# Attention in chunks of 120 keys with the global keys beside them, ahead of a squared-ReLU MLP, with TensorE's order written by hand

## The chip, the cores and the metric

The kernel runs on one core of a Trainium2 chip. The metric is the device time of one execution in microseconds; lower is better. A core has engines with an instruction row each: TensorE (PE; its weight loads are shown apart as PEld), VectorE (DVE), ScalarE (ACT), GpSimd (POOL) and SyncE (SP, which here only issues transfers). A matmul takes its operands from the on-chip memory SBUF, with the contraction on the 128 partitions, and writes to one of eight PSUM banks of 512 fp32 columns; the other engines carry results back to SBUF.

## The reference

Attention with a band of 32 keys on either side of each query and 8 global tokens that see every key and that every query sees, then an MLP with a squared ReLU. 8 batches, 8 heads, 576 tokens, 64 dimensions a head; 4608 tokens, 512 model dimensions, 2048 hidden ones.

```python
scores = scale * np.matmul(q, k.transpose(0, 1, 3, 2))
pos = np.arange(S)
mask = np.abs(pos[:, None] - pos[None, :]) <= window      # 32
is_global[global_idx] = True                              # 8 of 576
mask = mask | is_global[:, None] | is_global[None, :]
scores = np.where(mask, scores, -1000000000.0)
attn = np.exp(scores - np.max(scores, axis=-1, keepdims=True))
attn = attn / (np.sum(attn, axis=-1, keepdims=True) + 1e-09)
x = np.matmul(attn, v).transpose(0, 2, 1, 3).reshape(B * S, H * D)
r = np.maximum(x @ w_in, 0.0)
out = (s * (r * r) + b) @ w_out
```

Inputs and output are fp32. Both kernels compute in bf16 with fp32 sums in PSUM, leave out the subtraction of the maximum, and split the last line in two: s is multiplied into w_out once, and b times the column sums of w_out is a row that is added to each output (`bias_row`).

## The kernel before

**Attention.** For each batch GpSimd issues transfers that cast q and k of all heads to bf16 copies in DRAM (`emit_scratch`, L157 and L161); SP then loads them with a transposing transfer as `qT` and `kT`, 128 rows for a pair of heads. GpSimd copies the 8 global columns of each, one column an instruction, by a register that holds the index (L294). v is loaded in fp32 in the natural order and cast on ScalarE into `vbf`, which has a 65th column of ones for the softmax's denominator.

A head is then worked by itself, on 64 of the 128 rows of the contraction: scores of the global keys against all queries (`pgk`, L311 to L313), scores of five chunks of 128 keys against a window of up to 192 queries and against the 8 global queries (`ps_s`, L327 and L332, two chunks to a PSUM tile), Exp on ScalarE (L315, L316, L338), the band mask on VectorE (L342), 13 value matmuls into `po` (L352 to L379), the denominator's row by Ln, spread to 64 rows by two matmuls with ones (L386, L390), Exp of its negative, the product on VectorE (L397). The results of the global queries stand in eight extra columns; GpSimd copies each over its token's column (L399, eight copies a head), and SP sends the head's 64 x 576 tile into `xT`, four tiles that hold x transposed for all 4608 tokens.

**MLP.** Chunks of 512 tokens, nine in all. A chunk has 20 units: 16 of the first layer, four matmuls of 512 columns each into `psh` (L216), with ReLU (L221) and square (L222) on VectorE into `g`; and four of the second layer, 16 matmuls into `pso` (L229), an addition of the bias row (L234) and the transfer out. After each head the code emits its share of the units whose tokens are there; in the text a chunk's tokens are there when the batch that ends them is through.

**Order.** The scheduler of the tile framework lays each engine's instructions in a row and sets the semaphores; an instruction that waits holds all behind it on its engine. `ps_m` has two banks for the units, `ps_a` two for scores, `ps_o` two tiles for values. The weights are loaded in 20 transfers and cast on VectorE after the first head (`prep_weights`), where TensorE also sums the columns of w_out in 16 fp32 matmuls (L188).

## Time and profile before

| | |
|---|---|
| three runs | 585.25, 587.22, 588.34 us; median 587.22 |
| the profiled execution | span 585.2 us from its first instruction to its last |
| TensorE | busy 492.7 us, 84%; 2968 matmuls on record |
| VectorE, ScalarE, GpSimd | 296.8, 228.3 and 226.2 us (51, 39 and 39%) |
| mean granted clock of TensorE | 0.942 of full speed |
| DMA | 51.52 MB, 88 GB/s over the span |

A busy share is an average over the span, and stages differ. The profile also gives the busy time in 40 slices and in any window, the clock that TensorE was granted there, each group of instructions with the idle time ahead of it and what ended that, and the chain of work that ended last, followed back from the last instruction.

### The profile page before, as it was taken

The page shows a single profiled execution, that of the slowest core. Times are in us where ns is not written, and L with a number is a line of the kernel's source. Part 1 is how long each engine was busy: PE and PEld are TensorE (multiplying, and loading weights), DVE is VectorE, ACT ScalarE, POOL GpSimd, SP SyncE. Part 2 cuts the span into 40 slices and gives each one's busy share as a digit, 9 for nine tenths or more (in the row PEclk, how much of TensorE's full clock was granted, in tenths as well). Part 3 has the DMA queues.
Part 4 walks back from the last instruction along what each step waited for, and adds up shares of the span by engine and source line. Part 5 has one row for each costly group of instructions (what it writes and reads, how often), then busy time and mean ns, then how long its engine had stood idle before and what let it go on. Part 6 is the DMA issues. An engine that isn't in the chain of part 4 may idle for free.

```text
span 585.2 us, 10109 instructions
## 1 busy us (share of the span) xinstructions
PE 492.7 (84%) x2968; PEld 230.8 (39%) x3016; DVE 296.8 (51%) x655; ACT 228.3 (39%) x473; POOL 226.2 (39%) x1061
## 2 busy tenths in 40 slices
PE   0147205986999999999999999999999999999997
PEld 0023102432444445444444444444444444444443
DVE  4314002332673576367537744763666367448481
ACT  2023101372454455455555545564455455420000
POOL 4938660277263255316433442553223113310000
PEclk9999656965999999999999999999989999999999
DMA  7999999566322422352243225122400100110101
GB/s 225 160 275 158 157 158 194 164 108 136 49 51 70 122 52 37 88 116 43 53 116 77 37 73 142 33 57 68 123 16 12 65 28 12 34 65 0 73 0 72
DMA packets 164166, 51.52 MB, mean 88 GB/s; under 512 B 152848, under 2 KB 156944, under 8 KB 163600
## 3 DMA queue, kind: packets, MB, share of 16 engines
q1 hardware_dynamic: 90032, 41.45, 28.8%
q0 software_dynamic: 74080, 9.44, 25.2%
q8 instruction: 23, 0.38, 0.3%
q14 instruction: 31, 0.25, 0.1%
HBM read 36.71 MB, written 18.87 MB: 95 GB/s over the span
## 4 chain that ended last, share of the span: by engine, by line
PE 65%; issue 13%; POOL 12%; DMA 3%; DVE 3%; ACT 2%; POOLq 1%; ACTq 0%
PE psh L216 22%; PE pso L229 19%; PE ps_s L327 6%; PE po L362 4%; POOL qsc L157 3%; PE po L386 3%; PE po L352 3%; PE pgk L311 2%; POOL ksc L161 2%; POOL qgT L294 2%; POOL stage L399 2%; POOL kgT L294 2%; DMA xT<-stage 2%; PE po L367 2%; PE po L379 1%
## 5 line engine op out<-in xcount | busy, mean ns | idle before, releaser
L399 POOL COPY stage<-stage 64x1 bf16 x512 | 111.0, 217 | 200.5 <-DVE stage L397 172.5
L216 PE MATMUL psh<-xT,win_t 128*128 128x512 bf16 x545 | 159.3, 390 | 9.3 <-DMA xT<-stage 6.4
L229 PE MATMUL pso<-wout_t,g 128*128 128x512 bf16 x559 | 135.9, 380 | 0.2
L221 DVE TENSOR_SCALAR g<-psh 128x512 bf16<-128x512 f32 x144 | 97.8, 686 | 55.2 <-PE psh L216 53.8
L385 ACT ACTIVATE rsb<-po 1x584 bf16<-1x584 f32 x64 | 41.5, 648 | 122.9 <-PE po L379 122.6
L338 ACT ACTIVATE e<-ps_s 128x368 bf16<-128x368 f32 (+2 forms) x192 | 73.3, 407 | 40.5 <-PE ps_s L332 35.8
L342 DVE TENSOR_TENSOR emc<-e,m 128x368 bf16<-128x368 bf16 (+2 forms) x192 | 53.8, 304 | 59.5 <-ACT e L338 56.2
L229 PEld LDWEIGHTS <-g 128*128 128x128 bf16 x576 | 52.9, 98 | 61.0 <-issue 8.0
L216 PEld LDWEIGHTS <-win_t 128*128 128x128 bf16 x576 | 47.8, 98 | 60.1 <-issue 26.1
L397 DVE TENSOR_TENSOR stage<-po,rep 64x584 bf16<-64x584 f32 x64 | 48.5, 758 | 36.4 <-ACT rep L395 23.4
L315 ACT ACTIVATE egk<-pgk 8x512 bf16<-8x512 f32 x64 | 37.5, 587 | 71.8 <-PE pgk L311 41.0
L234 DVE TENSOR_TENSOR osb<-pso,bias_row 128x512 f32<-128x512 f32 x36 | 24.9, 692 | 78.5 <-PE pso L229 76.4
L294 POOL COPY qgT<-qT 128x1 bf16 x256 | 41.0, 316 | 60.7 <-DMA qT<-qsc 42.8
L327 PE MATMUL ps_s<-qT,kT 64*128 64x192 bf16 (+2 forms) x320 | 57.7, 244 | 5.4 <-ACT e L338 3.2
L222 DVE TENSOR_TENSOR g<-g 128x512 bf16<-128x512 bf16 x144 | 57.6, 418 | 1.9
L362 PE MATMUL po<-emc,vbf 128*65 128x160 bf16 (+2 forms) x320 | 47.9, 240 | 1.1 <-DVE emc L342 1.1
L327 PEld LDWEIGHTS <-kT 64*128 64x128 bf16 (+1 forms) x320 | 31.2, 98 | 43.5 <-issue 40.8
L395 ACT ACTIVATE rep<-po 64x584 bf16<-64x584 f32 x64 | 41.7, 652 | 16.9 <-PE po L390 15.9
L188 PE MATMUL ps_b<-wt,onesf 128*128 128x512 f32 x32 | 21.8, 834 | 30.3 <-DMA wt<-in_moe_w_out_dram 30.3
L311 PE MATMUL pgk<-qT,kgT 64*8 64x512 bf16 x64 | 25.5, 399 | 24.2 <-POOL kgT L294 23.7
L332 PE MATMUL ps_s<-qgT,kT 64*128 64x8 bf16 (+1 forms) x320 | 45.5, 169 | 0.0
L362 PEld LDWEIGHTS <-vbf 128*65 128x65 bf16 (+1 forms) x320 | 33.3, 114 | 30.3 <-issue 10.0
(56 smaller groups left out, 441.9 us busy)
## 6 DMA issues: line engine op xcount, KB each, us to landing
out_dram<-osb SPq DMA_DIRECT2D x36, 256.0 KB, 2.1
vnat<-in_v_dram SPq DMA_DIRECT2D x32, 256.0 KB, 4.3
xT<-stage SPq DMA_DIRECT2D x64, 72.0 KB, 2.0
wt<-in_moe_w_in_dram SPq DMA_DIRECT2D x4, 1024.0 KB, 7.9
wt<-in_moe_w_out_dram SPq DMA_DIRECT2D x16, 256.0 KB, 3.1
qsc<-in_q_dram POOLq DMA_DIRECT2D x7, 576.0 KB, 10.9
ksc<-in_k_dram POOLq DMA_DIRECT2D x7, 576.0 KB, 11.9
vnat<-in_v_dram SPq DMA_DIRECT2D x8, 128.0 KB, 4.9
```

The source lines that it names most:

```text
L216: nc.tensor.matmul(psh[:], win_t[:, a, f * P : f * P + P], xT[a][:, c0 : c0 + 512], start=(a == 0), stop=(a == 3),)
L221: nc.vector.tensor_scalar_max(g[:], psh[:], 0.0)
L222: nc.vector.tensor_mul(g[:], g[:], g[:])
L229: nc.tensor.matmul(pso[:], gT[f][:, uu * P : uu * P + P], wout_t[:, f], start=(f == 0), stop=(f == 15),)
L294: nc.gpsimd.tensor_copy(out=dstG[:, i : i + 1], in_=dstT[:, ds(greg_p[i], 1)])
L327: nc.tensor.matmul(ps_s[: MC[c], off : off + WN[c]], kT[r : r + D, P * c : P * c + MC[c]], qT[r : r + D, WLO[c] : WHI[c]],)
L332: nc.tensor.matmul(ps_s[: MC[c], off + WN[c] : off + WN[c] + NG], kT[r : r + D, P * c : P * c + MC[c]], qgT[r : r + D, :],)
L338: nc.scalar.activation(e[:nr, :tot], ps_s[:nr, :tot], AF.Exp, scale=SCALE)
L342: nc.vector.tensor_mul(emc[:nr, :tot], e[:nr, :tot], bmask[gi][:nr, :tot])
L362: nc.tensor.matmul(po[:65, lo:hi], VX(c), EM(c, 0, hi - lo), start=False, stop=(c == NCH - 1),)
L397: nc.vector.tensor_mul(stage[0:64, :], po[0:64, :], rep[64:128, :])
L399: nc.gpsimd.tensor_copy(out=stage[0:64, ds(greg_p[i], 1)], in_=stage[0:64, S + i : S + i + 1],)
```

## The change

**Keys.** A chunk is now 120 keys of the band and, in rows 120 to 127, the 8 global keys, so that a batch has 5 x 128 = 640 columns (`LQ`). The queries lie in the same 640 columns: 60, the 8 global ones, 60. The tokens' rows come from fp32 loads in the natural order (`load`, five transfers for a half batch of each of q, k, v); the global rows of all batches are gathered once into DRAM (`gather`, 24 transfers on ScalarE's queue) and copied in by one transfer a half batch (`fill_globals`). No copy of q or k goes by DRAM in bf16, and there is no transposing transfer.

**Casts and transposes.** GpSimd casts k, q and v (`cast`; in batch 0 VectorE casts k and q). TensorE transposes a pair of heads, 5 + 5 matmuls against the identity (`trans_k`, `trans_q`), and VectorE copies the result to SBUF. The queries' copy goes into a block-diagonal tile: head 0 in rows 0 to 63 and columns 0 to 639, head 1 in rows 64 to 127 and columns 640 to 1279, zeros elsewhere, so that one matmul gives a chunk's scores for both heads on all 128 rows of the contraction.

**Values and norm.** The five score tiles of a pair (`pss`) share two banks with the transposes (`pst`). `vx` has 64 columns of ones beside each head's values, so that the denominators stand in 64 rows of `po`; Ln and Exp go over 64 x 1280 at once, and no matmul spreads them. `po` takes three banks, one tile for all pairs. The global queries' parts are added over the five chunks (`gsum`), and GpSimd copies them over their tokens' columns once a batch, eight copies of four pairs each (`finish_batch`).

**MLP.** `xt` is a tile for each batch, three in turn. A chunk that straddles two batches takes its columns from two tiles, with two matmuls where there was one. ReLU moves to ScalarE (L428), the square stays on VectorE. The units have three banks. Weights come in 8 transfers of 1 MB; GpSimd casts and scales them and sums w_out's tiles, and one matmul sums its columns (L481).

**Order.** TensorE's and SP's rows stand as the code is written. `Q` hands out the MLP in quanta (a unit of the first layer, or a quarter of one of the second), eight between the steps of a pair; a chunk is handed out during the batch after the one that ends it. So a batch's first two pairs lie beside the first layer and the last two beside the second.

```diff
-MC = [min(P, S - P * c) for c in range(NCH)]
-WLO = [max(0, P * c - WIN) for c in range(NCH)]
-WHI = [min(S, P * c + MC[c] + WIN) for c in range(NCH)]
-WN = [WHI[c] - WLO[c] for c in range(NCH)]
+KC = 120
+HB = 60
+LQ = NCH * P
+LO = [0] + [P * c - WIN for c in range(1, NCH)]
+HI = [P * c + P + WIN for c in range(NCH - 1)] + [LQ]
+W = [HI[c] - LO[c] for c in range(NCH)]
...
+    ctx.enter_context(tc.manual_schedule(engines={ET.PE, ET.SP}))
...
+    xtp = ctx.enter_context(tc.tile_pool(name="xtp", bufs=3))
+    dramp = ctx.enter_context(tc.tile_pool(name="dramp", bufs=1, space=bass.MemoryType.DRAM))
+    ps_s = ctx.enter_context(tc.tile_pool(name="ps_s", bufs=2, space=bass.MemoryType.PSUM))
+    ps_o = ctx.enter_context(tc.tile_pool(name="ps_o", bufs=1, space=bass.MemoryType.PSUM))
+    ps_m = ctx.enter_context(tc.tile_pool(name="ps_m", bufs=3, space=bass.MemoryType.PSUM))
...
+    def load(bi, t, h0, nh):
+        src = NATSRC[t]
+        d = nat_tile(t, h0 // HG)
+        a = h0 % HG
+        for c in range(NCH):
+            n = min(KC, S - KC * c)
+            nc.sync.dma_start(
+                out=d[0:n, c, a : a + nh],
+                in_=src[bi, h0 : h0 + nh, KC * c : KC * c + n].rearrange("h s d -> s h d"),
+            )
...
+    def gather(eng, t, regs):
+        for i in range(NG):
+            eng.dma_start(
+                out=gsc[t][:, i], in_=NATSRC[t][:, :, ds(regs[i], 1), :].rearrange("b h o d -> b (h o) d")
+            )
...
+    for t in ("k", "q", "v"):
+        gather(nc.scalar, t, greg_a)
+    for half in range(2):
+        for t in ("k", "q", "v"):
+            load(0, t, HG * half, HG)
+            fill_globals(nc.scalar, 0, t, half)
...
+    def cast(bi, half, eng_k, eng_q, eng_v):
+        kt, qt = cast_k[bi], cast_q[bi]
+        hs = slice(HG * half, HG * half + HG)
+        eng_k(out=kt[:, :, hs], in_=nat_tile("k", half)[:])
+        eng_q(out=qt[:, :, hs], in_=nat_tile("q", half)[:])
+        eng_v(out=vbufs[bi % NV][:, :, hs, 0:D], in_=nat_tile("v", half)[:])
...
+    def trans_k(p):
+        bi, hp = divmod(p, 4)
+        ps = ps_s.tile([P, LQ], BF16, tag="s", name="pst")
+        src = cast_k[bi].rearrange("p c h d -> p c (h d)")
+        for c in range(NCH):
+            nc.tensor.transpose(
+                ps[:, P * c : P * c + P], src[:, c, P * hp : P * hp + P], ident[:]
+            )
+        kt = ktp.tile([P, LQ], BF16, tag="kt", name="kt")
+        nc.vector.tensor_copy(out=kt[:], in_=ps[:])
+        ktile[p] = kt
...
+    def trans_q(p):
+        bi, hp = divmod(p, 4)
...
+        qt = qbufs[p % NQ]
+        for hh in range(2):
+            r = slice(D * hh, D * hh + D)
+            nc.vector.tensor_copy(
+                out=halves(qt[r, hh]),
+                in_=ps[r].rearrange("p (c j) -> p c j", c=NCH)[:, :, 0:KC].rearrange(
+                    "p c (a j) -> p c a j", a=2
+                ),
+            )
+            nc.vector.tensor_copy(
+                out=qt[r, hh].rearrange("p (c j) -> p c j", c=NCH)[:, :, HB : HB + NG],
+                in_=ps[r].rearrange("p (c j) -> p c j", c=NCH)[:, :, KC:P],
+            )
...
+    def qk(p, c):
+        kt, qt = ktile[p], qbufs[p % NQ]
+        ps = ps_s.tile([P, 2, W[c]], FP32, tag="s", name="pss")
+        nc.tensor.matmul(
+            ps[:], kt[:, P * c : P * c + P], qt[:, :, LO[c] : HI[c]]
+        )
+        e = emp.tile([P, 2, W[c]], BF16, tag="e", name="e", bufs=3)
+        nc.scalar.activation(e[:], ps[:], AF.Exp, scale=SCALE)
+        em = emp.tile([P, 2, W[c]], BF16, tag=f"em{c}", name=f"em{c}")
+        nc.vector.tensor_mul(em[:], e[:], masks[c][:])
+        emt[(p, c)] = em
...
+        po = ps_o.tile([P, 2 * LQ], FP32, tag="o", name="po")
+        started = set()
+        for hh in range(2):
+            for c in range(NCH):
+                lo, hi = LO[c], HI[c]
+                while lo < hi:
+                    a = hh * LQ + lo
+                    bank = a // 512
+                    n = min(hi - lo, 512 * (bank + 1) - a)
+                    nc.tensor.matmul(
+                        po[:, a : a + n], vx[:, c, 2 * hp + hh, :],
+                        emt[(p, c)][:, hh, lo - LO[c] : lo - LO[c] + n],
+                        start=bank not in started, stop=(hh == 1 or c == NCH - 1),
+                        skip_group_check=True,
+                    )
+                    started.add(bank)
+                    lo += n
...
+    def norm(p):
+        bi, hp = divmod(p, 4)
+        po = otile[p]
+        xt, gs = xts[bi], gsums[bi]
+        ln = nrm.tile([P, 2 * LQ], FP32, tag="ln", name="ln", bufs=1)
+        nc.scalar.activation(ln[D:P], po[D:P], AF.Ln)
+        rep = nrm.tile([P, 2 * LQ], FP32, tag="rep", name="rep")
+        nc.scalar.activation(rep[D:P], ln[D:P], AF.Exp, scale=-1.0)
+        nc.vector.tensor_reduce(
+            out=gs[:, hp],
+            in_=po.rearrange("p (h c j) -> p h j c", h=2, c=NCH)[:, :, HB : HB + NG, :],
+            axis=AX.X, op=OP.add,
+        )
+        for hh in range(2):
+            nc.vector.tensor_tensor(
+                out=xt[D * hh : D * hh + D, hp].rearrange("p (c a j) -> p c a j", c=NCH, a=2),
+                in0=halves(po[0:D, hh * LQ : hh * LQ + LQ]),
+                in1=halves(rep[D:P, hh * LQ : hh * LQ + LQ]), op=OP.mult,
+            )
+    def finish_batch(bi):
+        xt, gs = xts[bi], gsums[bi]
+        rec = nrm.tile([P, 4, 2, NG], FP32, tag="rec", name="rec", bufs=1)
+        nc.vector.reciprocal(out=rec[0:D], in_=gs[D:P])
+        xg = nrm.tile([P, 4, NG], BF16, tag="xg", name="xg", bufs=2)
+        for hh in range(2):
+            nc.vector.tensor_tensor(
+                out=xg[D * hh : D * hh + D], in0=gs[0:D, :, hh], in1=rec[0:D, :, hh],
+                op=OP.mult,
+            )
+        for i in range(NG):
+            nc.gpsimd.tensor_copy(
+                out=xt[:, :, ds(greg_p[i], 1)], in_=xg[:, :, i : i + 1]
+            )
...
+            for f in range(16):
+                psh = ps_m.tile([P, 512], FP32, tag="moe", name="psh")
+                for a in range(4):
+                    for j, (bi, x0, d0, n) in enumerate(pieces):
+                        nc.tensor.matmul(
+                            psh[:, d0 : d0 + n], win_t[:, a, f * P : f * P + P],
+                            xts[bi][:, a, x0 : x0 + n],
+                            start=(a == 0 and j == 0), stop=(a == 3),
+                            skip_group_check=True,
+                        )
+                r = mop.tile([P, 512], BF16, tag="r", name="r")
+                nc.scalar.activation(r[:], psh[:], AF.Relu)
+                g = gpa.tile([P, 512], BF16, tag=f"g{f}", name=f"g{f}")
+                nc.vector.tensor_mul(g[:], r[:], r[:])
+                gl.append(g)
+                yield
+            for u in range(4):
+                pso = ps_m.tile([P, DM], FP32, tag="moe", name="pso")
+                for f in range(16):
+                    nc.tensor.matmul(
+                        pso[:], gl[f][:, u * P : u * P + P], wout_t[:, f],
+                        start=(f == 0), stop=(f == 15),
+                    )
+                    if f % 4 == 3 and f < 15:
+                        yield
+                osb = mop.tile([P, DM], FP32, tag="osb", name="osb")
+                nc.vector.tensor_add(out=osb[:], in0=pso[:], in1=bias_row[:])
+                nc.sync.dma_start(out=out[c0 + u * P : c0 + u * P + P, :], in_=osb[:])
+                yield
+    moe = moe_quanta()
+    moe_left = [0]
+    def Q(n=1):
+        for _ in range(n):
+            if moe_left[0] > 0:
+                next(moe)
+                moe_left[0] -= 1
...
+        for j in range(4):
+            wt = wtmp.tile([P, 4, 512], FP32, tag="w", name="wi")
+            nc.sync.dma_start(out=wt[:], in_=w_in2[:, :, 512 * j : 512 * j + 512])
+            nc.gpsimd.tensor_copy(out=win_t[:, :, 512 * j : 512 * j + 512], in_=wt[:])
...
+        for j in range(4):
+            wt = wtmp.tile([P, 4, DM], FP32, tag="w", name="wo")
+            nc.sync.dma_start(out=wt[:], in_=w_out2[:, 4 * j : 4 * j + 4])
+            nc.gpsimd.tensor_scalar_mul(
+                out=wout_t[:, 4 * j : 4 * j + 4], in0=wt[:], scalar1=s_bc[:]
+            )
+            for i in range(4):
+                if j == 0 and i == 0:
+                    nc.gpsimd.tensor_copy(out=wsum[:], in_=wt[:, 0])
+                else:
+                    nc.gpsimd.tensor_add(out=wsum[:], in0=wsum[:], in1=wt[:, i])
...
+    def prefetch(bi):
+        alloc_cast(bi)
+        for half in range(2):
+            for t in ("k", "q", "v"):
+                load(bi, t, HG * half, HG)
+                fill_globals(nc.sync, bi, t, half)
...
+    alloc_cast(0)
+    cast(0, 0, nc.vector.tensor_copy, nc.vector.tensor_copy, nc.gpsimd.tensor_copy)
+    cast(0, 1, nc.vector.tensor_copy, nc.vector.tensor_copy, nc.gpsimd.tensor_copy)
+    load_w()
+    prefetch(1)
+    trans_k(0)
+    trans_q(0)
+    for p in range(4 * B):
+        bi, hp = divmod(p, 4)
+        if hp == 0:
+            xts[bi] = xtp.tile([P, 4, 2 * HB * NCH], BF16, tag="xt", name="xt")
+            gsums[bi] = nrm.tile([P, 4, 2, NG], FP32, tag="gs", name="gs")
+        if hp in (1, 2) and bi + 1 < B:
+            g = nc.gpsimd.tensor_copy
+            cast(bi + 1, hp - 1, g, g, g)
+            if hp == 2 and bi + 2 < B:
+                prefetch(bi + 2)
+        qk(p, 0)
+        Q()
+        qk(p, 1)
+        Q()
+        qk(p, 2)
+        Q()
+        qk(p, 3)
+        Q()
+        qk(p, 4)
+        Q()
+        if p + 1 < 4 * B:
+            trans_k(p + 1)
+            Q()
+            trans_q(p + 1)
+        pv(p)
+        norm(p)
+        Q(2)
+        if hp == 3:
+            finish_batch(bi)
+            if bi == 0:
+                bias()
+            moe_left[0] = 32 * (((bi + 1) * S) // 512) - 32 * ((bi * S) // 512) + moe_left[0]
+    Q(moe_left[0])
+    wtmp_cm.__exit__(None, None, None)
```

GpSimd's row at the program's start. `win_t`, `wout_t` and `wsum` are the weights, `natk`, `natq` and `natv` the loaded fp32 tiles of keys, queries and values, `kb` and `qb` the cast ones of batch 1, `vx_401` the values of batch 0. Now, behind four casts of `wi` into `win_t`:

```order
L470 TENSOR_SCALAR wout_t<-wo,s_bc 128x2048
L475 COPY wsum<-wo 128x512
L477 TENSOR_TENSOR wsum<-wsum,wo 128x512 x2
L470 TENSOR_SCALAR wout_t<-wo,s_bc 128x2048
L477 TENSOR_TENSOR wsum<-wsum,wo 128x512 x5
L287 CAST vx_401<-natv_109 128x5x4x64
L470 TENSOR_SCALAR wout_t<-wo,s_bc 128x2048
L477 TENSOR_TENSOR wsum<-wsum,wo 128x512 x3
L470 TENSOR_SCALAR wout_t<-wo,s_bc 128x2048
L287 CAST vx_401<-natv_111 128x5x4x64
L477 TENSOR_TENSOR wsum<-wsum,wo 128x512 x5
L285 CAST kb<-natk_101 128x5x256
```

Before, GpSimd's row at that place, ahead of the first copies of global columns (`qgT`):

```order
L161 DMA ksc_272<-in_k_dram 576x2x64
L157 DMA qsc_271<-in_q_dram 576x2x64
L161 DMA ksc_272<-in_k_dram 576x2x64
L157 DMA qsc_315<-in_q_dram 4608x1x64
L161 DMA ksc_316<-in_k_dram 4608x1x64
L157 DMA qsc_1017<-in_q_dram 4608x1x64
L294 ISA
L294 COPY qgT_341<-qT_339 128x1
```

Weight work has moved to GpSimd, and the casts that TensorE's first value matmuls and the next batch need stand behind it; the issues of casting transfers are gone.

TensorE's row at a batch's end, where the next chunk's first unit comes. `xt_521` is the x of the batch that ends the part before, `xt_863` that of the batch just done. Now:

```order
L436 LDWEIGHTS g15_1150
L436 MATMUL pso_1353<-wout_t_325,g15_1150 128x512
L334 LDWEIGHTS kt_1364
L334 MATMUL pss_1428<-qbd2_411,kt_1364 128x320
L421 LDWEIGHTS win_t_324
L421 MATMUL psh_1434<-xt_521,win_t_324 128x64
L421 LDWEIGHTS win_t_324
L421 MATMUL psh_1434<-xt_863,win_t_324 128x448
```

Before, at such a place (`xT0_281` is rows 0 to 127 of x transposed for all tokens, `ps_vg` the global values of the next batch):

```order
L268 LDWEIGHTS sel_258
L268 MATMUL ps_vg_2697<-vbf_2692,sel_258 8x512
L311 LDWEIGHTS kgT_2708
L311 MATMUL pgk1_2793<-qT_2705,kgT_2708 8x512
L312 LDWEIGHTS kgT_2708
L312 MATMUL pgk2_2794<-qT_2705,kgT_2708 8x64
L313 LDWEIGHTS kgT_2708
L313 MATMUL pgk2_2794<-qgT_2707,kgT_2708 8x8
L216 LDWEIGHTS win_t_285
L216 MATMUL psh_2857<-xT0_281,win_t_285 128x512
```

The unit's 512 columns are cut in 64 and 448, and one score matmul stands between the last quantum of the old chunk and the first unit of the new one, where three matmuls of the global keys stood.

ScalarE's row from one first-layer pair to the next, now:

```order
L338 ACTIVATE e<-pss 128x320
L428 ACTIVATE r<-psh 128x512 x2
L372 ACTIVATE ln<-po 64x1280
L428 ACTIVATE r<-psh 128x512
L374 ACTIVATE rep<-ln 64x1280
L428 ACTIVATE r<-psh 128x512
L338 ACTIVATE e<-pss 128x320
```

Before, from one head to the next:

```order
L338 ACTIVATE e<-ps_s 128x368
L338 ACTIVATE e<-ps_s 128x400
L338 ACTIVATE e<-ps_s 64x104
L385 ACTIVATE rsb<-po 1x584
L315 ACTIVATE egk<-pgk_2393 8x512
L395 ACTIVATE rep<-po 64x584
L316 ACTIVATE egk<-pgk_2394 8x72
L338 ACTIVATE e<-ps_s 128x368
```

The ReLUs of the units stand now between the score tiles' Exps and between the Ln and the Exp of the norm.

## Rows read from the trace of the kernel before

**Rows 1.** The page: busy us by engine; GB/s in 40 slices.
```profile
PE 492.7 (84%) x2968; PEld 230.8 (39%) x3016; DVE 296.8 (51%) x655; ACT 228.3 (39%) x473; POOL 226.2 (39%) x1061
...
GB/s 225 160 275 158 157 158 194 164 108 136 49 51 70 122 52 37 88 116 43 53 116 77 37 73 142 33 57 68 123 16 12 65 28 12 34 65 0 73 0 72
```

**Rows 2.** The page: the chain that ended last, shares of the span.
```profile
PE 65%; issue 13%; POOL 12%; DMA 3%; DVE 3%; ACT 2%; POOLq 1%; ACTq 0%
```

**Rows 3.** Windows: length, busy us (count) of PE PEld DVE ACT POOL; clock, DMA, GB/s.
```profile
0.00:60.00 60.00, 20.91 (x90) 9.07 (x90) 20.19 (x52) 13.15 (x25) 41.00 (x95) 1.00 1.71 203
60.00:141.30 81.30, 43.27 (x218) 20.42 (x219) 17.14 (x42) 23.56 (x48) 41.83 (x192) 0.65 1.30 153
251.40:305.30 53.90, 52.72 (x350) 25.25 (x355) 32.29 (x71) 27.83 (x59) 22.68 (x128) 1.00 0.32 75
523.80:581.20 57.40, 56.08 (x245) 24.15 (x248) 35.90 (x72) 0.00 (x0) 0.00 (x0) 1.00 0.10 37
```

**Rows 4.** The chain in order of time: start us, us, what.
```profile
195.06 1.98 DMA xT<-stage
...
249.23 2.37 DMA xT<-stage
...
570.62 10.54 PE pso L229 x48
```

**Rows 5.** Timeline of PE near 338 us: start us, us, line, operation, tiles.
```profile
338.26 0.24 PE L327 MATMUL ps_s<-qT,kT 64*128 64x192 bf16 x1
...
338.36 0.24 PE L327 MATMUL ps_s<-qT,kT 64*128 64x192 bf16 x1
338.44 0.16 PE L332 MATMUL ps_s<-qgT,kT 64*128 64x8 bf16 x1
338.47 0.24 PE L327 MATMUL ps_s<-qT,kT 64*128 64x192 bf16 x1
```

**Rows 6.** Lines by form: busy us, mean ns | idle before, releaser.
```profile
L338 ACT ACTIVATE e<-ps_s 128x400 bf16<-128x400 f32 x64 | 32.0, 500 | 20.3 <-PE ps_s L332 18.8 <-DVE emc L342 1.4
L338 ACT ACTIVATE e<-ps_s 64x104 bf16<-64x104 f32 x64 | 15.9, 249 | 9.7 <-PE ps_s L332 7.1 <-DVE emc L342 0.6
L315 ACT ACTIVATE egk<-pgk 8x512 bf16<-8x512 f32 x64 | 37.5, 587 | 71.8 <-PE pgk L311 41.0 <-PE pgk L313 30.3
L395 ACT ACTIVATE rep<-po 64x584 bf16<-64x584 f32 x64 | 41.7, 652 | 16.9 <-PE po L390 15.9
L342 DVE TENSOR_TENSOR emc<-e,m 128x400 bf16<-128x400 bf16 x64 | 23.2, 363 | 5.8 <-ACT e L338 5.2
L397 DVE TENSOR_TENSOR stage<-po,rep 64x584 bf16<-64x584 f32 x64 | 48.5, 758 | 36.4 <-ACT rep L395 23.4 <-issue 9.9 <-POOL kgT L294 2.3
L222 DVE TENSOR_TENSOR g<-g 128x512 bf16<-128x512 bf16 x144 | 57.6, 418 | 1.9
L399 POOL COPY stage<-stage 64x1 bf16 x512 | 111.0, 217 | 200.5 <-DVE stage L397 172.5 <-POOL stage L399 0.8
```

**Rows 7.** Windows around a stretch with few matmuls, columns as in rows 3.
```profile
63.60:94.20 30.60, 1.04 (x2) 0.50 (x2) 0.49 (x2) 0.00 (x0) 15.20 (x29) 0.50 2.25 179
94.20:97.70 3.50, 3.50 (x6) 1.42 (x5) 1.31 (x4) 0.00 (x0) 0.00 (x0) 0.50 0.28 92
97.80:101.00 3.20, 2.60 (x21) 1.44 (x20) 0.47 (x2) 1.96 (x4) 0.00 (x0) 1.00 0.69 195
```

**Rows 8.** Lines by form: GpSimd's mask selects.
```profile
L126 POOL TENSOR_SCALAR_AFFINE_SELECT m<-m 128x192 bf16<-128x192 bf16 x3 | 1.0, 364 | 0.0
...
L121 POOL TENSOR_SCALAR_AFFINE_SELECT m<-m 128x96 bf16<-128x96 bf16 x1 | 0.3, 290 | 0.0
```

**Rows 9.** The start: chain row, a DMA issue (KB, us to landing), SP timeline row.
```profile
7.77 0.29 POOLq L91
...
wt<-in_moe_w_in_dram SPq DMA_DIRECT2D x2, 1024.0 KB, 6.7
...
0.82 0.40 SPq L82 DMA_DIRECT2D gidx_i<-in_global_idx_dram  x1
```

More of the change, by code (lines that the diff above doesn't have):

```diff
@@ new lines, with fill_globals @@
+    gsc = {
+        t: dramp.tile([B, NG, H, D], FP32, name=f"gsc{t}", tag=f"gsc{t}")
+        for t in ("k", "q", "v")
+    }
+    def gather(eng, t, regs):
[3 more added lines that the diff above has]
+            )
+    def fill_globals(eng, bi, t, half):
+        d = nat_tile(t, half)
+        src = gsc[t][bi, :, HG * half : HG * half + HG].rearrange("g h d -> g (h d)")
+        src = bass.AP(
+            tensor=src.tensor, offset=src.offset,
+            ap=[list(src.ap[0]), [0, NCH], list(src.ap[1])],
+        )
+        eng.dma_start(
+            out=d[KC:P].rearrange("p c h d -> p c (h d)"), in_=src
+        )
@@ new lines @@
+    greg_a = [
+        nc.scalar.value_load(g32[:1, i, 0:1], min_val=0, max_val=S - 1) for i in range(NG)
+    ]
+    greg_p = [
+        nc.gpsimd.value_load(g32[:1, i, 0:1], min_val=0, max_val=S - 1) for i in range(NG)
+    ]
+    for t in ("k", "q", "v"):
[4 more added lines that the diff above has]
+            fill_globals(nc.scalar, 0, t, half)
+    s_bc = const.tile([P, 1], FP32)
+    nc.sync.dma_start(out=s_bc[:], in_=_bcast_dram(moe_s[:], P))
@@ L90 @@
[L90 to L98 removed]
+    WM = P + 2 * WIN
+    iot = const.tile([P, WM], FP32)
+    rowi = const.tile([P, 1], FP32)
+    nc.gpsimd.iota(
+        iot[:], pattern=[[1, WM]], base=-WIN, channel_multiplier=0,
+        allow_small_or_imprecise_dtypes=True,
+    )
@@ L99 @@
+    nc.vector.tensor_scalar(
+        out=kidx[:], in0=kidx[:], scalar1=rowi[:], scalar2=None, op0=OP.add
+    )
+    vkey = const.tile([P, NCH], FP32)
+    nc.vector.tensor_scalar(
+        out=vkey[:], in0=kidx[:], scalar1=float(S) - 0.5, scalar2=ngrow[:],
+        op0=OP.is_le, op1=OP.mult,
+    )
     notg = const.tile([P, NCH], FP32)
@@ L102 @@
         nc.vector.scalar_tensor_tensor(
[L103 removed]
+            out=notg[:], in0=kidx[:], scalar=gidx_f[:, i : i + 1], in1=notg[:],
             op0=OP.is_equal, op1=OP.add,
@@ new lines, in bias @@
+    def bias():
+        ps = ps_m.tile([P, DM], FP32, tag="moe", name="psb")
+        nc.tensor.matmul(ps[:], onesf[:], wsum[:])
+        nc.vector.tensor_scalar_mul(out=bias_row[:], in0=ps[:], scalar1=b_bc[:])
+    def prefetch(bi):
+        alloc_cast(bi)
+        for half in range(2):
+            for t in ("k", "q", "v"):
+                load(bi, t, HG * half, HG)
+                fill_globals(nc.sync, bi, t, half)
+    alloc_cast(0)
+    cast(0, 0, nc.vector.tensor_copy, nc.vector.tensor_copy, nc.gpsimd.tensor_copy)
```

427 lines of the change are left out of this document (133 added, 294 removed).

## The prediction

> **What bounds the kernel now.** I read the page's busy shares first, then the chain that ended last, then windows by stage. TensorE is busy 492.7 of 585.2 us, VectorE 51%, ScalarE and GpSimd 39% each [rows 1]; 65% of the chain is TensorE work, 12% GpSimd, 3% DMA [rows 2]. The share hides three stages. To 141.3 us TensorE has little to do: it is busy 20.9 us of the first 60 and 43.3 us of the next 81.3, much of that at the lower clock, while GpSimd prepares the casting DMAs and copies columns [rows 3]. Then come batches with a steady period: the wait for the last head's transfer into xT ends one batch at 195.06 + 1.98 = 197.0 and the next at 249.23 + 2.37 = 251.6, so about 54.5 us a batch, in which TensorE is busy 52.7 of 53.9 us [rows 3, 4]. From 523.8 to the last matmul at 581.2 only the two last chunks of the MLP run (57.4 us) and 4.0 us follow to the span's end [rows 3, 4]. So the start of 141 us is a wait, the rest is TensorE's instruction stream, and the reader should ask of the change: how long is the new start, how long is a batch, how long is the tail.
>
> **TensorE in a batch.** The MLP's matmuls stay: 128 of 512 columns per chunk, at the pace of the dense stretch, 48 in 10.54 us, 0.2196 us each [rows 4]: 28.1 us. The rest of 54.5 us, some 26 us, is now attention with 28 small matmuls a head. The new code has for a pair of heads 5 score matmuls (320, 384, 384, 384, 320 columns, 1792) and 14 for the values (1792 columns, four of the ten ranges cut at a bank), together 3584 columns: at 0.2196/512 us a column 1.54 us. What a small matmul costs beyond its columns I take from the score rows: 192 + 8 columns, two weight loads, start every 0.105 to 0.11 us, of which the columns are 0.086, so about 0.012 us for each of the two [rows 5]. 19 of them: 0.23 us. Ten transposes of 128 columns have no row of before; below, their columns and this overhead (0.055 + 0.012 = 0.067 us); above, no overlap at all, each as long as a whole recorded small matmul, 0.24 us [rows 5]. I take 0.067, since the score rows, the nearest, do overlap. A pair is then 1.54 + 0.23 + 0.67 = 2.44, four pairs 9.8 us. Chunks 1 to 7 straddle two batches, so each of their 64 first-layer matmuls is cut in two: 64 more, between 0.012 and 0.055 us each (a load that a 64-column matmul doesn't cover); at 0.03, 1.9 us (chunk 0, in one of the seven batches, is not cut; neglected). Stream: 28.1 + 9.8 + 1.9 = 39.8 us a batch.
>
> **What else TensorE waits for in a batch.** ScalarE takes, for each of the five score tiles, an Exp: from 104 to 400 columns an Exp grows from 249 to 500 ns, 0.85 ns a column [rows 6]; so 320 and 384 columns cost 0.43 and 0.49 us, five of them 2.3 us; Ln and Exp over 1280 columns go from 652 ns at 584 [rows 6] to 1.24 us each; Relu of 512, which comes over from VectorE, like the Exp of 512, 0.59. A pair with eight first-layer units costs ScalarE 2.3 + 2.5 + 4.7 = 9.5 us, against 10.4 us of TensorE: eight units of 4 x 0.2196 = 0.88, the pair's 2.44, and 32 cut matmuls at 0.03. VectorE: five masks at 0.32 to 0.36 (363 ns at 400 columns), one PSUM copy of 640 and two of 600 by the 758 ns of the 584-column product (0.8 each), two such products (1.55), four small ones (0.7), eight squares at 0.418: 9.7 us [rows 6]. Both fit, barely. TensorE is held where Ln, two Relus and the reciprocal's Exp stand in one row on ScalarE (4.1 us with the next pair's first Exp): going through units and score matmuls in order, the second unit of the next pair waits 0.8 us for its PSUM bank, in the two pairs of each batch with first-layer units: 1.6 us. The fourth output sum of a chunk keeps one of the three MLP banks until half a batch later, where a unit waits for an Exp, a mask and an addition: about 1 us.
>
> **The batch's end.** A new chunk's first unit needs the last pair's columns of xt and then the eight GpSimd copies that replace the global ones. Behind the last value matmul lie Ln 1.24, Exp 1.24, two products 1.55, and eight copies, now 217 ns each [rows 6], with gaps 2.1: 6.1, with handovers 6.5 us. TensorE has two units and one score matmul to cover it, 1.9 us. Queued behind the blocked matmul is all of TensorE's stream, so 4.6 us are idle. Then the clock: in the 30.6 us with two matmuls it stood at 0.50, and dense work from 94.2 to 97.7 was still at 0.50 (1.2 GHz), the stretch behind it at 1.00 (2.4 GHz) [rows 7]. If each end drops it, 3.5 us at half speed lose 1.7 us; bounds 0 and 1.7, I take 1.7. A batch: 39.8 + 1.6 + 1.0 + 4.6 + 1.7 = 48.7 us; seven: 341.
>
> **The start.** GpSimd now casts the weights, and behind them in its row stand the casts of batch 0's values and batch 1's keys. Its price for 2048 fp32 elements is not in the trace. Its only wide operation, the mask select, takes 290 ns at 96 and 364 at 192 columns [rows 8]: by that slope, 0.77 ns, 1.8 us; by the 96-column row without a fixed part, 3.0 ns, 6.2 us. I take 2.7 us, nearer to the slope, since a fixed part plainly exists, with 0.9 for 512 and 1.75 for 1280. The Trainium skill, "GPSIMD Engine Reference", section 3.1, gives 4497 ns for a two-source add of 2048 fp32 elements, about 1.1 us for 512; by it the 16 adds cost 3 us more and the total 3 us; no run shows it yet.
> Steps: the registers of the eight indices are read till about 8.1 us [rows 9]; 24 gathers and six fills at 0.5 (0.40 issue and a gap) land by 26; the 30 loads, 3.5 MB at the first slice's 225 GB/s [rows 1], take 16 us from 4 on, so the first weight tile is issued at about 23 and, at 6.7 us a tile [rows 9], lands at 30. With two buffers: casts till 32.7 and 35.4, the next pair lands 39.5 and 42.2, casts till 44.9, the first output tiles land 49 and 51.7; scaling, copy, adds till 61.6; value cast 63.4: the first pair's value matmuls. Then two more tiles and eight adds, with the other value cast at 74.5, till 79; keys and queries of batch 1 till 82.5. TensorE's row has pair 3's value matmuls behind the transposes of batch 1, so they end at 86; norm and copies: 94. The attention of batch 0 lies under this. First unit at 94 (now 143); by 1.8 us a tile the same steps give 83, by 6.2 us 132.
>
> **Tail and sum.** 57.4 of now, 1.9 for the cut matmuls of chunk 7, 4.0 behind, rounded up: 64 us; what the Relu on ScalarE may give there is left out. 94 + 341 + 64 = 499 us of span. The profiled execution's span was 585.2 and the three runs 585.25 to 588.34, median 587.22, 2.0 above it: 501.
>
> **Rivals.**
> A, the batch's end hardly stalls and ScalarE's row does not hold TensorE: for it, ScalarE is busy only 28 of 53.9 us now [rows 3]; against it, the xt dependency is of the whole tile. 39.8 + 1 + 2 = 42.8 a batch: 460 us.
> B, transposes don't overlap: 0.24 each instead of 0.067, 40 a batch, 6.9 us, seven batches 48: 549 us. For it, no transpose is in the trace; against it, score matmuls with as many weight loads do overlap [rows 5]. The Trainium skill, "TensorE: Matmul & The Clock Gate", Part 4, tells of about 275 ns for a 128x128 transpose in one kernel; by it 559 us; no row here shows it.
> C, GpSimd at its upper price: start 132, 539 us. For it, the small rows; against it, the slope.
> D, slower: the two score banks. Every score matmul and transpose takes one of two, and both leave by way of ScalarE or VectorE rows in which a Relu or a copy stands ahead. If that closes a loop, so that each of the 16 first-layer units waits for its own Relu and Exp (0.59 + 0.46) instead of running beside them, a batch gets 16 x 1.05 = 16.8 us longer: 619 us. It decides at 12.3 us a batch, 0.77 us a unit, (587 - 501) / 7. For it, ScalarE and VectorE at 9.5 and 9.7 of 10.4 us; against it, one unit lies between any two score matmuls.
> E, no net change: start at its upper end, 38 us more, and D's loop at 7 us a batch instead of 16.8, 49 us more: 588 us.
>
> **Numbers.** Forecast 0.57, A 0.15, B 0.10, C 0.07, D 0.08, E 0.03. The time is the forecast's, 501 us; its own range, with the bounds of start (83 to 132) and clock, is 478 to 540. From 455, which takes in A, to 558, which takes in B and C, D and the far ends are left out. About 0.5% is what a measurement can tell from no change here: faster 0.89, same 0.03, slower 0.08.
>
> **What would show it.** The first unit of the first layer at 83 to 132 us, with GpSimd's casts the last thing in front of it; batches 46 to 51 us apart; TensorE idle 4 to 5 us at each end, released by GpSimd's xt copies, with a lower clock behind it; transposes starting 0.06 to 0.08 us apart; a Relu of 0.59, a Ln of 1.24 us. Wrong it would be by waits for pss or pst inside pairs of more than 1 us, by weight casts over 4 us, or by loads of the next batch that come late, which now show no wait.

## The result and the profile after

The changed kernel takes 486.61 us (median of four runs, 483.66 to 487.83) against 587.78 for the kernel before on the same chip: a ratio of 0.828, with a 95% interval of 0.824 to 0.832. Forecast were 501 us, in a range of 455 to 558.

The page of the kernel after, busy time by engine and the chain that ended last; they answer to [rows 1, 2]:

```profile
PE 353.8 (73%) x2503; PEld 212.4 (44%) x2530; DVE 293.5 (60%) x672; ACT 230.8 (47%) x369; POOL 129.8 (27%) x155
...
PE 34%; issue 26%; POOL 10%; DMA 10%; ACT 7%; SPq 6%; DVE 5%; ACTq 1%; POOLq 1%; DVEq 0%
```

TensorE is busy 139 us less and is still the longest, but only 34% of the chain is now its work. The windows of the kernel after, cut where each new chunk's first unit starts (columns as in [rows 3]):

```profile
0.00:60.00 60.00, 4.84 (x25) 2.45 (x25) 29.84 (x62) 3.52 (x6) 31.77 (x32) 1.00 0.77 175
60.00:106.14 46.14, 19.04 (x104) 11.18 (x105) 27.45 (x52) 17.15 (x24) 37.48 (x30) 1.00 0.98 174
106.14:151.81 45.67, 38.05 (x241) 20.50 (x246) 32.84 (x74) 27.11 (x44) 10.82 (x15) 0.98 0.70 106
151.81:203.09 51.28, 41.35 (x306) 23.13 (x308) 33.76 (x75) 27.56 (x44) 12.08 (x16) 0.90 0.45 80
203.09:248.17 45.08, 39.33 (x305) 24.61 (x308) 30.17 (x75) 27.46 (x44) 10.51 (x15) 0.95 0.71 121
248.17:292.59 44.42, 38.69 (x305) 26.03 (x308) 30.88 (x75) 27.34 (x44) 9.29 (x14) 0.96 0.67 118
```

The start is 106.1 us (forecast 94). Seven batches follow, from 106.14 to 424.19, 45.4 us each (forecast 48.7): five between 44.4 and 45.7, one of 51.3 (the odd batch below) and the last of 42.2. From there to the span's end at 486.0 are 61.8 us (forecast 64). So the three terms were off by +12, -23 and -2 us.

A batch's end on TensorE's timeline, and the clock behind the end before it, at 248.17:

```profile
287.79 0.27 PE L421 MATMUL psh<-xt,win_t 128*128 128x256 bf16 x1
292.59 1.08 PE L421 MATMUL psh<-xt,win_t 128*128 128x256 bf16 x7 [4.53 <-POOL xt L398]
```

```profile
248.17:251.60 3.43, 3.43 (x19) 2.35 (x19) 1.23 (x2) 1.25 (x3) 2.44 (x2) 0.60 1.16 166
251.60:255.00 3.40, 3.40 (x32) 2.67 (x30) 2.76 (x6) 2.67 (x7) 1.25 (x1) 0.90 1.09 270
255.00:260.00 5.00, 4.94 (x57) 4.13 (x55) 3.79 (x10) 3.89 (x5) 1.25 (x1) 1.00 0.09 34
```

The unit's first matmul needs the old batch's `xt` and runs; the second needs the new one and waits 4.53 us for GpSimd's copies. Then TensorE works without a gap but at a granted clock of 0.60 (mostly 1.2 of 2.4 GHz) and 0.90: 3.43 x 0.40 + 3.40 x 0.10 = 1.7 us lost. TensorE's waits over the whole run (total us, times, longest):

```profile
PE pst L300 <- DVE kb L285: 46.4, 1, 46.4
PE psh L421 <- POOL xt L398: 37.2, 8, 5.6
PE po L357 <- POOL vx L287: 12.1, 1, 12.1
PE pss L334 <- ACT e L338: 9.9, 17, 1.3
PE po L357 <- DVE em L340: 5.6, 7, 1.4
PE psh L421 <- ACT r L428: 3.6, 5, 0.7
PE pso L436 <- DVE osb L443: 3.3, 1, 3.3
```

At the start GpSimd's row runs nearly without a gap from the first output weights to batch 1's casts (timeline, start us, us):

```profile
46.49 5.45 POOL L470 TENSOR_SCALAR wout_t<-wo,s_bc 128x2048 bf16<-128x2048 f32 x1 [5.60 <-DMA wo<-in_moe_w_out_dram]
...
60.90 6.62 POOL L477 TENSOR_TENSOR wsum<-wsum,wo 128x512 f32<-128x512 f32 x5
67.46 1.25 POOL L287 CAST vx<-natv 128x1280 bf16<-128x1280 f32 x1
...
83.69 1.25 POOL L287 CAST vx<-natv 128x1280 bf16<-128x1280 f32 x1
84.90 6.74 POOL L477 TENSOR_TENSOR wsum<-wsum,wo 128x512 f32<-128x512 f32 x5
91.58 1.25 POOL L285 CAST kb<-natk 128x1280 bf16<-128x1280 f32 x1
...
104.05 2.04 POOL L398 COPY xt<-xg 128x4 bf16 x8 [7.40 <-DVE xt L381]
```

The first value matmuls, which wait for the cast at 67.46, start at 68.76, and the first unit 37.4 us later. From there to the copies TensorE waits no more for GpSimd, but for ScalarE's Exps (8.9 us) and VectorE's masks and copies (3.8). Three rows of its timeline:

```profile
68.76 1.68 PE L357 MATMUL po<-em,vx 128*128 128x160 bf16 x14 [12.07 <-POOL vx L287]
70.23 0.79 PE L334 MATMUL pss<-qbd,kt 128*128 128x320 bf16 x2
72.22 0.48 PE L334 MATMUL pss<-qbd,kt 128*128 128x384 bf16 x1 [1.20 <-ACT e L338]
```

Scaling 2048 columns takes 5.6 us, while the plain cast of as many (`L465`) takes 1.9.

### The profile page after: what moved, and what is told of

It reads as the page before. It is cut to its first block, busy times and chain, and to the rows that moved or that the text cites. A ratio compares the mean times of both kernels' runs of the same rounds, so it can differ in the third digit from the quotient of the medians.

```text
span 486.0 us, 7310 instructions
## 1 busy us (share of the span) xinstructions
PE 353.8 (73%) x2503; PEld 212.4 (44%) x2530; DVE 293.5 (60%) x672; ACT 230.8 (47%) x369; POOL 129.8 (27%) x155
## 4 chain that ended last, share of the span: by engine, by line
PE 34%; issue 26%; POOL 10%; DMA 10%; ACT 7%; SPq 6%; DVE 5%; ACTq 1%; POOLq 1%; DVEq 0%
PE psh L421 17%; PE pso L436 11%; SPq L124 5%; PE po L357 3%; ACT r L428 3%; POOL wout_t L470 2%; POOL xt L398 2%; DMA wi<-in_moe_w_in_dram 2%; ACT rep L374 2%; PE pss L334 2%; POOL wsum L477 2%; DMA wo<-in_moe_w_out_dram 2%; DVE xt L381 2%; POOL qb L286 2%; DMA natq<-in_q_dram 1%
## 5 line engine op out<-in xcount | busy, mean ns | idle before, releaser
L421 PE MATMUL psh<-xt,win_t 128*128 128x512 bf16 (+7 forms) x1020 | 155.7, 303 | 41.5 <-POOL xt L398 37.2
L421 PEld LDWEIGHTS <-win_t 128*128 128x128 bf16 x1024 | 91.6, 103 | 95.4 <-issue 57.9
L428 ACT ACTIVATE r<-psh 128x512 bf16<-128x512 f32 x144 | 86.4, 600 | 87.3 <-PE psh L421 81.9
L338 ACT ACTIVATE e<-pss 128x384 bf16<-128x384 f32 (+1 forms) x160 | 73.4, 471 | 79.7 <-DMA wo<-in_moe_w_out_dram 49.5
L430 DVE TENSOR_TENSOR g<-r 128x512 bf16<-128x512 bf16 x144 | 70.6, 490 | 62.5 <-ACT r L428 62.1
L340 DVE TENSOR_TENSOR em<-e,mask 128x384 bf16<-128x384 bf16 (+1 forms) x160 | 73.1, 477 | 8.0 <-ACT e L338 6.9
L372 ACT ACTIVATE ln<-po 64x1280 f32<-64x1280 f32 x32 | 39.4, 1232 | 69.7 <-PE po L357 69.7
L334 PE MATMUL pss<-qbd,kt 128*128 128x384 bf16 (+1 forms) x160 | 55.1, 352 | 12.0 <-ACT e L338 9.9
L381 DVE TENSOR_TENSOR xt<-po,rep 64x600 bf16<-64x600 f32 x64 | 49.6, 775 | 16.3 <-ACT rep L374 14.8
L357 PE MATMUL po<-em,vx 128*128 128x160 bf16 (+3 forms) x448 | 35.7, 228 | 17.7 <-POOL vx L287 12.1
L374 ACT ACTIVATE rep<-ln 64x1280 f32<-64x1280 f32 x32 | 40.5, 1267 | 0.9
L318 DVE COPY qbd<-pst 64x600 bf16<-64x600 bf16 x64 | 29.9, 466 | 11.8 <-PE pst L312 11.4
L334 PEld LDWEIGHTS <-kt 128*128 128x128 bf16 x160 | 16.5, 105 | 24.7 <-issue 12.1
```

Source lines behind the costliest of these rows:

```text
L318: nc.vector.tensor_copy(out=halves(qt[r, hh]), in_=ps[r].rearrange("p (c j) -> p c j", c=NCH)[:, :, 0:KC].rearrange("p c (a j) -> p c a j" ...
L334: nc.tensor.matmul(ps[:], kt[:, P * c : P * c + P], qt[:, :, LO[c] : HI[c]])
L338: nc.scalar.activation(e[:], ps[:], AF.Exp, scale=SCALE)
L340: nc.vector.tensor_mul(em[:], e[:], masks[c][:])
L357: nc.tensor.matmul(po[:, a : a + n], vx[:, c, 2 * hp + hh, :], emt[(p, c)][:, hh, lo - LO[c] : lo - LO[c] + n], start=bank not in started, ...
L372: nc.scalar.activation(ln[D:P], po[D:P], AF.Ln)
```

## Experiments

Each is an edit of the kernel after and is to be read against its 486.6 us. Times are medians of four runs; the kernel before took 587.2 to 587.5 beside them.

**The MLP one pair later.** The 32 quanta are released behind the next batch's first pair, so eight quanta of the old chunk cover a batch's end.

```diff
-            moe_left[0] = 32 * (((bi + 1) * S) // 512) - 32 * ((bi * S) // 512) + moe_left[0]
+            owed[0] = 32 * (((bi + 1) * S) // 512) - 32 * ((bi * S) // 512)
+        if hp == 0 or p == 4 * B - 1:
+            moe_left[0] += owed[0]
+            owed[0] = 0
```

> Each chunk's MLP is handed out one pair later, so that eight quanta of the old chunk (7 us of TensorE work) stand at each batch's end behind the last value matmuls. Theory (the batch's end costs 4.6 us of waiting for GpSimd's copies into xt and some 1.8 us at half clock behind it): seven ends save 6.2 us each, 43 us, and the first unit of all comes some 6 us later; 449 us, batches 38 to 39 us apart, no wait of psh for xt above 0.5 us. Rival (ScalarE and VectorE, busy 27 and 31 of 44 us, then set the pace, and the wait goes into the pairs as waits of pss and psh): batches 42 us apart, 468 us or more.

437.9 us, 49 less. Two windows of it, each a batch from one set of `xt` copies to the next:

```profile
221.30:259.60 38.30, 37.15 (x310) 25.16 (x308) 29.72 (x76) 27.35 (x44) 10.18 (x15) 1.00 0.68 124
259.60:298.10 38.50, 37.47 (x312) 26.41 (x310) 30.66 (x76) 27.24 (x44) 9.51 (x15) 1.00 0.72 128
```

No wait for `xt` is left among TensorE's waits, the clock of the profiled execution stays at 1.00 (0.984 to 0.992 in the other three), and a steady batch takes 38.4 us instead of 44.4, which is the 4.5 us of idle time and the 1.7 of clock. More was gained than I expected: the first unit starts at 105.1, no later than before, and the seven batches are 51.6 us shorter in the profiled execution, 7.4 each instead of 6.2; the odd one takes 43.1 instead of 51.3, where the clock had been 0.90. The rival (ScalarE and VectorE set the pace) is out: they are as busy as before, in fewer us.

**Only the clock.** 16 matmuls nobody reads, at six batch ends:

```diff
+                for i in range(16):
+                    nc.tensor.matmul(
+                        psd[:], wout_t[:, 0, 0:P], wout_t[:, i], start=(i == 0), stop=(i == 15)
+                    )
```

> At six batch ends (batches 1 to 6) 16 matmuls of 512 columns on weights alone, 3.5 us, whose result nobody reads, stand in TensorE's row ahead of the blocked unit, inside the 4.6 us of waiting. Theory (the half clock behind a batch's end comes from TensorE standing idle there, and costs 1.8 us each): 11 us less, 476 us, and the granted clock stays 1.00 behind the ends. Rival 1 (the low clock has nothing to do with the idle time): 487 us. Rival 2 (the extra tile takes one of three PSUM banks and holds units back): slower than 490 us.

480.8 us, 5.8 less (the profiled spans differ by 8.6). Behind an end of it:

```profile
246.30:249.80 3.50, 3.50 (x31) 2.77 (x31) 1.88 (x4) 2.40 (x5) 2.75 (x3) 1.00 1.17 169
```

31 matmuls run in 3.5 us at 1.00, where 19 ran at 0.60. The idle time does bring the clock down. The gain is half to three quarters of what I expected, and this run's trace shows two stretches at a granted clock of 0.50 (1.2 GHz) that the kernel after does not have: 4.7 us behind the first unit, an end that was not filled, and 3.4 us from 161.9 on, behind a wait of 2.5 us for a mask product. They lose 2.3 and 1.7 us.

**Transposes twice.** `for c in 2 * list(range(NCH))` in `trans_k` and `trans_q`.

> Every transpose is done twice into the same place. Theory (transposes overlap and lie on the path that sets the end: 0.056 us each by the trace, 40 a batch, seven batches): 2.2 us a batch more, 16 us in all, 503 us. Rival 1 (the waits of the batch take them up): under 5 us more. Rival 2 (a transpose costs as much as its recorded duration, 0.23 us): 9 us a batch, 65 us more, 550 us.

498.4 us, 11.8 more. TensorE's added work is on the path: steady batches take 47.5 us instead of 44.5. Of these 3.0 us some 0.9 is clock: in the 3.4 + 3.4 us behind the end at 248.3 us it is 0.50 and 0.74, against 0.60 and 0.90 in the kernel after. That leaves 2.1 us for 40 transposes, near the 2.2 expected. The start came out 2.7 us shorter (TensorE waits 6.5 instead of 12.1 us for the first values) and the odd batch 1.0, so less than 16 arrived at the end. 40 transposes at their recorded 0.23 us would have been 9 us a batch; rival B is out.

**Scaling on ScalarE.** `nc.scalar.activation(..., AF.Copy, scale=s_bc[:])` in place of GpSimd's four scalings.

> The four scalings of w_out (5.6 us each on GpSimd) go to ScalarE, nothing else moves. Theory (GpSimd's row sets the start): the first pair's value matmuls start near 59 us instead of 68.8, the first unit comes at 88 to 92 us instead of 106, and the time is 470 us. Rival (the loads of the weights through two buffers, or the chain of four pairs itself, set the start): first unit after 100 us, 480 us or more.

477.5 us, 9.1 less; first unit at 97.4. GpSimd's value casts now start at 56.8 instead of 67.5, with the 15 additions (20 us) still around them, and the first value matmuls at 58.3, as the theory has it. But the first unit comes 39.1 us behind these, where 29 to 33 were expected and 37.4 stood before; in ScalarE's row a scaling of 2.0 us now stands between a Ln and its Exp. So both theory and rival hold in part: GpSimd's row sets when the values come, and the four pairs of batch 0 set the rest.

**Global rows earlier.** ScalarE's 24 gathers take 28.6 us to issue; here each tensor's two transfers follow its own eight.

```diff
+    for t in ("k", "q", "v"):
+        gather(nc.scalar, t, greg_a)
+        for half in range(2):
+            fill_globals(nc.scalar, 0, t, half)
```

> At the start the six transfers of batch 0's global rows stand behind their own tensor's eight gathers in ScalarE's queue instead of behind all 24 (28.6 us of issues). Theory (TensorE's first 46 us of waiting for the key cast cost nothing, since GpSimd's row of weights and casts sets the first unit): first transposes near 24 to 35 us instead of 46.4, the first unit still at 105 to 107 us, 487 us. Rival (the late first scores push the four pairs of batch 0 and with them the first unit): first unit 8 us earlier or more, 478 us or less.

497.1 us, 10.5 more, which neither theory nor rival had. TensorE's timeline:

```profile
26.27 0.72 PE L300 MATMUL pst<-ident,kb 128*128 128x128 bf16 x5 [26.27 <-DVE kb L285]
...
82.52 1.68 PE L357 MATMUL po<-em,vx 128*128 128x160 bf16 x14 [31.46 <-POOL vx L287]
```

The first transposes come 20 us earlier. The scheduler has put both value casts behind the fourth scaling in GpSimd's row (81.2 instead of 67.5 us); the first value matmuls come 13.8 us later and the first unit 10.7 later, at 116.9. So it is again the row that sets when the values come. The 46 us of waiting for keys, TensorE's longest wait, hold nothing by themselves: in the kernel after 12.1 us of waiting for values follow them, and with the keys 20 us earlier that wait is 31.5 us. What the earlier transfers bring with the casts in their old order was not run.

**Start without both.** Scaling and batch 0's value casts on ScalarE, with the earlier transfers:

> Start alone: scalings of w_out and the value casts of batch 0 on ScalarE, the transfers of batch 0's global rows behind their own gathers. Theory (the first unit comes 34 to 36 us after the first value matmuls, and what holds these is GpSimd's row: 68.8 us as it is, 82.5 with the earlier transfers alone): with the value casts off that row the first value matmuls start near 50 us, the first unit near 87, 468 us. Rival (the four pairs of batch 0 or the loads hold it, as with the scalings alone, 97 us): 476 us or more.

479.6 us: the rival. The first unit comes at 96.7 for a new reason, a wait of 14.0 us:

```profile
57.99 0.86 PE L334 MATMUL pss<-qbd,kt 128*128 128x384 bf16 x2 [14.03 <-ACT e L338]
```

In ScalarE's row the last gathers, two casts and three scalings now stand ahead of the first Exp. The wait moved from one row to another, and the first unit comes 33 us behind the first value matmuls (63.4).

**Casts of later batches on ScalarE.** `g = nc.scalar.copy` for the casts of batches 1 to 7.

> The casts of batches 1 to 7 (six a batch, 1.3 us each) go from GpSimd to ScalarE. Theory (VectorE's products of two SBUF tiles take 1.1 to 1.4 us beside a GpSimd cast and 0.34 to 0.42 otherwise, but only the first batches feel it): behind the start every mask product is below 0.37 and every square below 0.43 us; GpSimd's row at the start ends 5 us earlier, first unit near 100 us; ScalarE gets 7 us more a batch, 35 of 44; 480 us. Rival 1 (the slow products cost 3 us in each batch): 465 us. Rival 2 (ScalarE becomes the bound and holds units back): 495 us or more.

501.2 us, 14.6 more: rival 2. ScalarE gets 35 of 48 us busy, TensorE's waits for Exp go from 9.9 to 17.7 us and steady batches take 45.6 to 48.4. The first unit comes at 106.2, not near 100, although the first value matmuls start 2.5 us earlier (66.2). Behind the start the slow products (last section) are gone, and the odd batch still takes 52.5 us, so they were not its cause.

**ReLU on VectorE.** `nc.vector.tensor_scalar_max(r[:], psh[:], 0.0)`.

> The ReLU goes back from ScalarE to VectorE, as it was before the change. Theory (VectorE then has some 15 us in each pair beside the first layer, against 9 us of TensorE): these pairs, two a batch, get 5 us longer, 540 to 570 us. Rival (VectorE has room, since it is busy 31 of 44 us in a batch): 500 us or less.

504.4 us, 17.8 more, between theory and rival. The waits, of which the first two are new or grown:

```profile
PE psh L421 <- DVE r L428: 16.2, 17, 1.6
PE pss L334 <- DVE qbd L324: 10.5, 11, 2.3
PE pss L334 <- ACT e L338: 6.8, 8, 1.3
```

VectorE does become the slowest engine beside the first layer, but a steady batch is 48, not 54 us: two thirds of the 5 us a pair do not arrive. What takes them up was not tried.

**Banks three and two** (`ps_s` bufs=3, `ps_m` bufs=2).

> Three PSUM banks for scores and transposes, two for units, instead of two and three. Theory (the two score banks hold TensorE little: 14 us of waits of pss and pst in all, half of them at the start under GpSimd's row, while two unit banks are held by late output sums): 490 to 505 us. Rival (the score banks set the pace of a pair): batches 3 us shorter, 470 us or less.

502.8 us, as the theory says: TensorE's waits for ReLU grow from 3.6 to 19.1 us (35 times), those of `pss` for Exp fall from 9.9 to 5.8. This edit gives the scores a bank and takes one from the units, so by itself it shows only that the trade loses. What puts rival D out is the kernel after: in its seven batches TensorE waits 3.1 us in all for an Exp ahead of `pss`, never more than 0.4, where D had 16.8 us in each batch.

**Both gains together**, with the bias matmul behind batch 1's first pair, then with the value gathers in GpSimd's queue:

> The start as in the run beside it, the MLP handed out one pair later, and the bias row's matmul behind batch 1's first pair. Theory (the two gains stand in different places and add): 437.9 less 18 to 20, 419 us. Rival (with the MLP a pair later the first unit no longer depends on the start's row): 430 us or more.

> As the run before, with the eight gathers of values and their two transfers in GpSimd's queue, so that ScalarE's queue holds 16 gathers instead of 24. Theory (an issue takes 1.1 to 1.4 us on ScalarE and the value casts wait for the last of 24): first value matmuls 6 us earlier, 413 us. Rival (queries' scores, not the values, hold the first pair, or GpSimd issues more slowly): same as the run before within 2 us.

429.9 and 425.0 us. In the first, at its rival's time, the 14 us wait of Exp remains (14.3), and 8 of the 18 to 20 us arrive. In the second that wait is 6.7 at most; the first value matmuls come 15 us earlier (48.4), but the first copies end only 6.6 us earlier, at 90.4 instead of 97.0, and the time lies between theory and rival. Then the sums over w_out on TensorE:

> As e11_best2, but the 16 sums over w_out leave GpSimd: TensorE sums the scaled bf16 tiles with 16 matmuls of ones behind the fourth pair's scores, and the row is multiplied by b/s. Theory (a weight buffer comes free only when GpSimd has added it, 20 us for the four, so ScalarE's later scalings wait for their load with the Exps of batch 0 behind them, 3.2 and 6.7 us of waits of pss in that run): these waits go below 2 us, the first batch's copies into xt end near 82 instead of 90.4 us, 417 us. Rival (the chain of four pairs goes on at 10 to 12 us a pair for other reasons): 423 us or more.

423.5 us, the rival. The waits of 3.4 and 6.9 us stay, and ScalarE's row shows that it was not the weight buffers but the scalings themselves, with the norm's Ln and Exp between them:

```profile
61.72 1.23 ACT L376 ACTIVATE ln<-po 64x1280 f32<-64x1280 f32 x1 [2.28 <-PE po L361]
62.98 2.00 ACT L475 ACTIVATE wout_t<-wo,s_bc 128x2048 bf16<-128x2048 f32 x1
65.00 1.27 ACT L378 ACTIVATE rep<-ln 64x1280 f32<-64x1280 f32 x1
66.62 2.00 ACT L475 ACTIVATE wout_t<-wo,s_bc 128x2048 bf16<-128x2048 f32 x1 [0.35 <-DMA wo<-in_moe_w_out_dram]
68.65 0.82 ACT L342 ACTIVATE e<-pss 128x320 bf16<-128x320 f32 x2
```

The first copies end at 92.0, no earlier than the 90.4 of the run before: the sums now stand in TensorE's row from 78.0 to 83.5 us, at a granted clock of 0.59. By its median it is the fastest version run, 0.721 of the kernel before (0.718 to 0.723), but the run before, at 0.725 (0.722 to 0.729), can't be told from it.

## Why the prediction was right, step by step

**The batch's end was right.** Forecast were 4.6 us idle and 1.7 of clock; the trace shows 4.53 and 1.7, and the two experiments separate them. It was called a term among five; it is all that lay between a steady batch's 44.4 and 38.4 us, and rival A was wrong.

**TensorE's stream was mis-sized**, 39.8 us a batch; it is 36.7 by the sum below, and TensorE is busy 37.2 to 37.5 in a batch with the MLP a pair later. I had charged each small matmul 0.012 us beyond its columns, from 64-row score rows, and each cut one 0.03. On the timeline of the kernel after:

```profile
168.63 1.04 PE L421 MATMUL psh<-xt,win_t 128*128 128x64 bf16 x8
169.51 0.30 PE L334 MATMUL pss<-qbd,kt 128*128 128x320 bf16 x1
169.64 1.04 PE L421 MATMUL psh<-xt,win_t 128*128 128x64 bf16 x8
170.52 0.44 PE L300 MATMUL pst<-ident,kb 128*128 128x128 bf16 x5
170.80 1.04 PE L421 MATMUL psh<-xt,win_t 128*128 128x64 bf16 x8
171.67 0.44 PE L312 MATMUL pst<-ident,qb 128*128 128x128 bf16 x5
171.95 0.98 PE L357 MATMUL po<-em,vx 128*128 128x160 bf16 x14
172.77 0.41 PE L421 MATMUL psh<-xt,win_t 128*128 128x64 bf16 x3
```

A cut unit of eight takes 0.88 us from start to start, as four uncut ones did (4 x 0.2196); five transposes 0.28, 0.056 each, their columns alone; the 14 value matmuls 0.82 instead of 0.94. Per pair 0.77 + 0.82 + 0.56 = 2.15 instead of 2.44; a batch 28.1 + 8.6 = 36.7. That is 3.1 us a batch less by the sum and 2.5 by the busy time, so some 17 of the 23 us; the two waits below are the rest. The Trainium skill, "TensorE: Matmul & The Clock Gate", Part 4, tells of about 275 ns for a transpose in one kernel; recorded durations here are 232 ns, but the starts are 56 ns apart, and the time goes by the starts.

**ScalarE's row and the late output sum** were put at 1.6 and 1.0 us a batch, 18 us in seven. In the seven batches TensorE waits 12.8 us for all but `xt`: 3.6 for ReLU, 3.3 for an output sum, 3.1 for Exps and 2.6 for masks. ReLU took 0.60 and Ln 1.23 us as forecast; the three unit banks hid most, since with two the wait for ReLU is 19.1. The output sum came once, in the batch of 51.3, where three output additions stand in a row in VectorE's order behind a pair's norm, and the clock falls behind it (0.50 from 187.4 to 190.8). In that batch SP's row, in the order in which it was written, also holds the next loads behind four output transfers from 156 to 188 us, and GpSimd waits 33.5 us for them, though TensorE waits for none of their casts. Why the scheduler stacks the additions there was not tried.

**The start** failed at two steps. The first is GpSimd's prices: the first value matmuls were forecast at 63.4 us and come at 68.8, 5 of the 12 us. Ahead of them stand two scalings, put at 2.7 us each by the slope of the mask selects and measured at 5.6, near the upper bound of 6.2 that rival C took for every operation, and seven additions at 1.27 instead of 0.9: 8 us more. The first output weights came 2.5 us sooner than forecast (46.5), and the copy (0.61 instead of 0.9) and the value cast (1.25 instead of 1.75) were cheaper. The Trainium skill's figure for an addition ("GPSIMD Engine Reference", section 3.1), some 1.1 us as an estimate, was nearer than mine. The second step is "The attention of batch 0 lies under this". It does not: GpSimd's casts are through at 96.6, 7.4 us before the copies, and no matmul behind the first values waits for them. It is the chain of four pairs that takes 37.4 us from the first value matmuls to the first unit, where the forecast had 30.6; the value matmuls of these pairs start 7.9 to 10.4 us apart. In the experiments that stretch is 33 to 45 us, whatever GpSimd's row is. The gathers were off as well, 28.6 us of issues instead of 12, but the wait for the values stands behind them.

**Signs.** The idle time at each end, its releaser, the lower clock behind it, ReLU and Ln came as foretold. Steady batches lie 44.4 to 45.7 us apart instead of 46 to 51, transposes start 0.056 us apart instead of 0.06 to 0.08, and what stands ahead of the first unit is the four pairs, not GpSimd's casts. Of the signs of being wrong, the price over 4 us came with the scalings of w_out.

So the sum came nearer than its terms, since the start's error and the stream's had opposite signs: that the time is within 3% of 501 us is in part luck.
